# Sketched attention and a two-layer feed-forward stage: a list scheduler that counts SBUF port conflicts and shifts due times, and key features in four column tiles

## The chip, the cores and the metric

The program runs on one core of a Trainium2 chip (trn2). The metric is the device time of one execution in microseconds (us); the kernel before has a median of 130.67 us over 3 runs (130.46 to 130.88). Engines are named as the profile names them: PE is TensorE (PEld its weight loads), DVE is VectorE, ACT is ScalarE, POOL is GpSimd, SP is SyncE, which issues the DMAs.

## The reference

Attention without a softmax: queries and keys go through two 8x32 sketches S1 and S2, and the 64 features of a row are all products of the two sketched vectors. Keys and values are summed into a 64x32 matrix per head, and queries are multiplied by it and divided by the same product with the sum of the key features. The result, 4352 rows of 128, goes through a feed-forward stage of width 2048 whose activation is linear on both sides of zero.

```python
batch, n_heads, seq, head_dim = (4, 4, 1088, 32)      # r = 8
def phi(x):
    a = np.einsum('rd,bhsd->bhsr', S1, x)
    b = np.einsum('rd,bhsd->bhsr', S2, x)
    return np.einsum('bhsi,bhsj->bhsij', a, b).reshape(*x.shape[:-1], r * r)
kv  = np.einsum('bhsf,bhsd->bhfd', phi(k), v)
z   = np.sum(phi(k), axis=2)
num = np.einsum('bhsf,bhfd->bhsd', phi(q), kv)
den = np.einsum('bhsf,bhf->bhs', phi(q), z)[..., None] + 1e-06
x   = (num / den).transpose(0, 2, 1, 3).reshape(4352, 128)
h   = x @ w_in                                        # 128 x 2048
out = (np.maximum(h, 0) + alpha * np.minimum(h, 0)) @ w_out
```

The kernel rewrites the last line: with w_b = alpha * w_out and w_a = w_out - w_b, the output is relu(h) @ w_a + x @ W, where W = w_in @ w_b.

## The kernel before, in words

The kernel doesn't issue its work in program order. It first collects some hundreds of operations (`Op`, L35: a candidate engine or several, a planned duration in ns, operations it depends on, buffers it holds, a due time), then `plan` (L54) orders them, and the loop at L766 emits them in the planned order. Each engine runs its own list strictly in that order; semaphores between engines are put in where data or buffers need them, and nowhere else.

`plan` works backwards once: an operation's due time is at most that of each user, less 1.6 times its duration and latency (L62 to L64). Then it goes forwards: among the operations whose inputs are placed and whose buffers can be had, it takes on each engine the one with the earliest due time that can start within a few hundred ns (`AHEAD`) of the earliest start, and of these the one that starts first. Two engines never hinder each other in this plan, except by data and buffers.

Stages, by the names and lines that matter here:

- **Dummies.** Five matmuls on zeros (`warm`, L343) start the PE. Until the first matmul of the feed-forward stage is due, the emitting loop also fills planned gaps on the PE with such dummies, one for each 216 ns of gap less 150 ns (L769).
- **Keys** (`keys`, L485, and `kfeat`, L442), four batches, each in two halves of two heads. A half's keys are transposed (batch 0 on PE, L451; the others on DVE, L493), the features a and b come from four matmuls with the transposed keys as 128x128 weights and the block-diagonal sketches as 64 moving columns (`fe`, L460, operation "ab"), they are copied from PSUM to SBUF ("abc", L221 on ACT or L223 on DVE), and their products ("kp", L473) are formed on POOL, or on DVE for the first half of batch 0 and for the two sets of the last 64 rows (`k_rest`, L478). Then `kv` (L506: 32 matmuls with 32-column weights, L513, and small ones, L521) and `kvr` (L524) sum keys times values, and `zm`, `fin`, `zz` (L538 to L562) make kvW and zc.
- **Queries** (`queries`, L566), four batches and the last rows ("qr"): a DVE transpose (L570), two rounds of 16 matmuls (L584), copies by ACT (aq), products on DVE (L597), then denominators and numerators (L611), a transpose (L620), eps and reciprocal (`rc`, L626 and L627), a transpose (L629) and the product that gives xT (L634). Batch 0 does this in two parts, so that the feed-forward stage can start on the first.
- **Weights** (L387 to L434): w_in is cast to bf16 in four pieces; for each of four pieces of w_out, w_b is made on ACT (L404) or POOL (L395), w_a on POOL (L395), a bf16 copy of w_b ("w_hi", L223) and its remainder ("w_lo", L395) on DVE; winT (L420) and 32 matmuls (`Wmm`, L431) give W.
- **Feed-forward** (`mlp`, L685), eight groups of 512 rows and a last one of 256 (the last rows of all batches): for each of 16 chunks a matmul h (L694), a relu from PSUM to bf16 on ACT (L700) or DVE (L702), and a matmul o (L712) that accumulates in PSUM bank 7; at the end W (L708) into the same bank, an output transpose (L718, for the last group L730) and stores by SP. h takes at most four PSUM banks, the relu outputs eight buffers. Group g is due at 17 us + g * 10.2 us, chunk c of it 0.64 us later each.

DMA loads are issued by SP in one fixed order (L296 to L314): k0, q0, v0, the last rows of k and v of batches 0 and 1, k1, w_in, w_out, and then the other batches.

Of the kernel before, what the change touches and what calls it, by code (L numbers as in the profile page):

```python
# [25 lines left out]
class Buf:  # L26
# [3 lines left out]
    def __init__(self, cls, n=1, stream=None, most=99, prefer=None):  # L30
        self.cls, self.n, self.stream, self.most, self.prefer = cls, n, stream or cls, most, prefer
        self.slot, self.users, self.last = None, 0, 0.0


class Op:  # L35
    def __init__(self, eng, dur, emit, deps=(), bufs=(), lat=0, due=1e9, name=""):
        self.eng = (eng,) if isinstance(eng, str) else tuple(eng)
        self.dur = dur if isinstance(dur, dict) else {e: dur for e in self.eng}
        self.emit, self.bufs, self.lat, self.due, self.name = emit, list(bufs), lat, due, name
        self.deps = [d for d in deps if d is not None]  # L40
        self.start = self.end = self.on = None
        self.arrive = 0.0
        for b in self.bufs:
            b.users += 1
# [6 lines left out]
AHEAD = {"pe": 120, "act": 150, "dve": 250, "pool": 300, "sp": 0}  # L51


def plan(ops, classes):  # L54

    free_at = {e: 0.0 for o in ops for e in o.eng}
    freed = {c: [0.0] * n for c, n in classes.items()}
    held = {c: [False] * n for c, n in classes.items()}  # L60
    holds = {b.stream: 0 for o in ops for b in o.bufs}
    for o in reversed(ops):  # L62
        for d in o.deps:
            d.due = min(d.due, o.due - STRETCH * (min(d.dur.values()) + (0 if d.eng == o.eng == ("pe",) else d.lat + SEM)))  # L64
    waiting = sorted(ops, key=lambda o: o.due)
    order = []

    def place(o, ready):
# [24 lines left out]

    while waiting:
        shut, can = set(), []
        for o in waiting:
            new = {b.stream for b in o.bufs if b.slot is None}
            no = new & shut or any(d.end is None for d in o.deps)
            shut |= new
            if no:  # L100
                continue
            at, picks = place(o, min(max([free_at[e]] + [d.end for d in o.deps]) for e in o.eng))
            if picks is None:
                continue
            fits = []
            for e in o.eng:
                t = max([at, free_at[e]] + [d.end + SEM if d.on != e else d.free if e == "pe" else d.end + OWN for d in o.deps])
                fits.append((t + o.dur[e] * BIAS.get(e, 1), t, e))
            _, t, e = min(fits)
            end = t + o.dur[e]  # L110
            can.append((t, e, o, end, picks))
        assert can
        first, best = {}, {}
        for c in can:
            first[c[1]] = min(first.get(c[1], 1e18), c[0])
        for c in can:
            if c[0] <= first[c[1]] + AHEAD[c[1]]:
                best.setdefault(c[1], c)
        t, e, o, end, picks = min(best.values(), key=lambda c: c[0])
        for b, i in picks:  # L120
            b.slot = i
            holds[b.stream] += b.n
            for j in range(i, i + b.n):
                held[b.cls][j] = True
        o.free = end
        o.start, o.end, o.on = t, max(end + o.lat, o.arrive), e
        free_at[e] = end
        for b in o.bufs:
            b.users -= 1
            b.last = max(b.last, o.end)  # L130
            if not b.users:
                holds[b.stream] -= b.n
                for j in range(b.slot, b.slot + b.n):
                    held[b.cls][j] = False
                    freed[b.cls][j] = b.last + SEM
        waiting.remove(o)
        order.append(o)
    return sorted(order, key=lambda o: o.start)
# [3 lines left out]
def kernel(  # L142
# [52 lines left out]
    def ps(b):  # L195
        return PS[:, b.slot] if b.n == 1 else PS[:, b.slot:b.slot + b.n]
# [8 lines left out]
    def op(*a, **kw):  # L205
        o = Op(*a, **kw)
        ops.append(o)
        return o
# [107 lines left out]
    def got(name):  # L316
        return loads[name]
# [69 lines left out]
    for i in range(NP):  # L387
        s = slice(CP * i, CP * i + CP)

        def wc(e, s=s):  # L390
            copy(e, w_in_bf[:, s.start * 128:s.stop * 128], w_in_f[:, s.start * 128:s.stop * 128])
        c_win.append(op(("act", "dve"), {"act": 615, "dve": 350}, wc, got("w_in"), name="w_in_bf"))

    def tt(out, a, b, what):
        return lambda e: (nc.vector if e == "dve" else nc.gpsimd).tensor_tensor(out=out, in0=a, in1=b, op=what)  # L395
# [1 line left out]
    for i in range(NP):  # L397
        s = slice(CP * i, CP * i + CP)
        al = bview(alphaT[:, s], [[1, CP], [0, DM]])

        def wbe(e, s=s, al=al):
            if e == "act":
                for c in range(s.start, s.stop):
                    nc.scalar.activation(w_b_f[:, c], w_out_f[:, c], ACTF.Copy, scale=alphaT[:, c:c + 1])  # L404
            else:
                tt(w_b_f[:, s], w_out_f[:, s], al, ALU.mult)(e)
        wb = op(("act", "pool"), {"act": 1560, **big}, wbe, [c_S] + got("w_out"), name="w_b")
        c_wa.append(op("pool", big, tt(w_a_bf[:, s], w_out_f[:, s], w_b_f[:, s], ALU.subtract), [wb], name="w_a"))
        hi = op(("act", "dve"), {"act": 615, "dve": 350}, lambda e, s=s: copy(e, w_hl[:, 0, s], w_b_f[:, s]), [wb], name="w_hi")
        c_lo.append(op(("dve", "pool"), big, tt(w_hl[:, 1, s], w_b_f[:, s], w_hl[:, 0, s], ALU.subtract), [hi], name="w_lo"))  # L410
    for i in range(2):
        b = ph()
        s = slice(8 * i, 8 * i + 8)
# [28 lines left out]
    def kfeat(srcs, needs, due, ab_t, kp_t, bab, bkp, kp_eng, tag, turn=None):  # L442
# [14 lines left out]

        def fe(e):
            for j in range(n):
                nc.tensor.matmul(ps(bf)[:, j * 64:(j + 1) * 64], sb(bT)[:, j * 128:(j + 1) * 128],  # L460
                                 S12blk.rearrange("p h c -> p (h c)"), start=True, stop=True)
        o = op("pe", 225 * n, fe, [o, c_S], [bT, bf], 200, due + 2, tag + "ab")
        o = op(("act", "dve"), ad(64 * n),
               lambda e: copy(e, bview(ab_t(), [[r, n * H], [r * n * H, 2], [1, r]]),
                              bview(ps(bf), [[2 * r, n * H], [r, 2], [1, r]])), [o], [bf] + bab, LA, due + 3, tag + "abc")
# [1 line left out]
        def pr(e):  # L467
            a = ab_t()
            m = n * H
            dst = bview(kp_t(), [[R, m], [r, r], [1, r]])  # L470
            i0 = bview(a, [[r, m], [1, r], [0, r]])
            i1 = bass.AP(tensor=a.tensor, offset=a.offset + r * m, ap=[list(a.ap[0]), [r, m], [0, r], [1, r]])
            (nc.vector if e == "dve" else nc.gpsimd).tensor_tensor(out=dst, in0=i0, in1=i1, op=ALU.mult)  # L473
        return op(kp_eng, {"dve": dv(256 * n), "pool": 110 + 256 * n * 1.8}, pr, [o], bab + bkp, 80, due + 4, tag + "kp")

    rest_k = [None, None]

# [7 lines left out]
    def keys(b, due, kp_eng):  # L485
# [52 lines left out]
        def zm(e):  # L538
# [3 lines left out]
                                 bview(H4, [[1, 4], [0, r]]))  # L542
            nc.vector.tensor_reduce(out=u, in_=bview(t, [[1, r], [r, 4]]), axis=AX.X, op=ALU.add)
            nc.vector.tensor_mul(bview(w, [[r, H], [1, r]]), bview(u, [[0, H], [1, r]]), bview(mask4, [[1, H], [0, r]]))
        o1 = op("dve", 300, zm, [o, c_mask2], [bk, bz], 80, due + 31, f"zm{b}")
        o2 = op(("act", "dve"), ad(128), lambda e: copy(e, sb(bs), bview(ps(bk), [[0, 2], [1, R]])), [o1], [bk, bs], LA,
                due + 32, f"kvc{b}")

# [17 lines left out]
    def queries(tag, needs, due, qsrc, nf, moving, bs, nums, ncol, xmul, bx, parts=1):  # L566
# [34 lines left out]
        for part in range(parts):  # L601
# [21 lines left out]
            def rc(e, dt=dt, nb=nb):  # L623
# [1 line left out]
                u = sb(dt)[:, :nb, 1]  # L625
                nc.vector.tensor_scalar_add(t, t, EPS)  # L626
                nc.vector.reciprocal(u, t)  # L627
            o = op("dve", 250 + 8 * nb / 0.96, rc, [o], [dt], 80, name=tag + "rc")
            o = op("dve", dv(nn), lambda e, dt=dt, rr=rr, nn=nn, nb=nb: nc.vector.transpose(  # L629
                sb(rr)[:, :nn], bview(sb(dt)[:, :, 1], [[32, nb], [0, 32]])), [o], [dt, rr], 80, name=tag + "rr")  # L630
            for g in range(2) if parts == 1 else [part]:
# [134 lines left out]
    for o in done:  # L766
        if o.on == "pe":
            if o.start < first:
                dummy(max(0, int((o.start - t - 150) / 216)))  # L769
            t = o.start + o.dur["pe"]  # L770
        o.emit(o.on)

# [29 lines left out]
```

## Time and profile before

| | us |
|---|---|
| median of 3 runs | 130.67 (130.46 to 130.88) |
| the profiled execution, its own time | 131.18 |
| span in its profile | 129.4 |
| PE busy | 112.9 (87%) |
| PEld busy | 54.3 (42%) |
| DVE busy | 83.6 (65%) |
| ACT busy | 79.4 (61%) |
| POOL busy | 22.7 (18%) |

The profiled execution takes 1.78 us more than its span, and 0.51 us more than the median. Busy times are sums over instructions; a matmul counts as busy from its start to its modelled end, so matmuls that follow each other closely overlap in them. In the chain that ended last, PE has 69% of the span and DVE 17%. The time runs in three parts: the head, in which loads, features and the first queries are worked through until the first h matmul at 22.65 us; the feed-forward stage, with the keys and queries of later batches in between, until 122 us; and the last output and its store, until 129.4 us.

### The profile page before, as it was taken

The page shows a single profiled execution, that of the slowest core. Times are in us where ns is not written, and L with a number is a line of the kernel's source. Part 1 is how long each engine was busy: PE and PEld are TensorE (multiplying, and loading weights), DVE is VectorE, ACT ScalarE, POOL GpSimd, SP SyncE. Part 2 cuts the span into 40 slices and gives each one's busy share as a digit, 9 for nine tenths or more (in the row PEclk, how much of TensorE's full clock was granted, in tenths as well). Part 3 has the DMA queues.
Part 4 walks back from the last instruction along what each step waited for, and adds up shares of the span by engine and source line. Part 5 has one row for each costly group of instructions (what it writes and reads, how often), then busy time and mean ns, then how long its engine had stood idle before and what let it go on. Part 6 is the DMA issues. An engine that isn't in the chain of part 4 may idle for free.

```text
span 129.4 us, 3045 instructions
## 1 busy us (share of the span) xinstructions
PE 112.9 (87%) x1212; PEld 54.3 (42%) x1228; DVE 83.6 (65%) x148; ACT 79.4 (61%) x157; POOL 22.7 (18%) x20
## 2 busy tenths in 40 slices
PE   6997993980999999999999999999999999998800
PEld 2565371350763543355353253643233433445500
DVE  3174799999984789785665884265987535566300
ACT  3335274593078459568887568884766888765610
POOL 3025029992000083000006006000000000000000
PEclk9999998599599999999999999999999999999975
DMA  3999995699900022022004001300040310401300
GB/s 117 258 308 359 298 273 101 211 283 326 189 12 3 5 49 35 0 45 42 0 4 82 1 0 29 57 0 0 11 75 0 60 23 0 84 3 25 61 14 26
DMA packets 32322, 11.22 MB, mean 87 GB/s; under 512 B 26788, under 2 KB 31668, under 8 KB 32180
## 3 DMA queue, kind: packets, MB, share of 16 engines
q1 hardware_dynamic: 32196, 11.01, 35.1%
q8 instruction: 9, 0.15, 0.5%
q14 instruction: 5, 0.04, 0.1%
q10 hardware_dynamic: 112, 0.02, 0.1%
HBM read 8.80 MB, written 2.23 MB: 85 GB/s over the span
## 4 chain that ended last, share of the span: by engine, by line
PE 69%; DVE 17%; ACT 5%; issue 2%; POOL 2%; DVEq 0%; ACTq 0%
PE ps L712 20%; PE ps L694 20%; PE ps L584 6%; PE ps L611 6%; PE ps L460 5%; PE ps L513 4%; DVE aq__76 L597 4%; DVE w_hl L223 3%; PE ps L342 3%; POOL kp__71 L473 2%; DVE w_hl L395 2%; ACT rh__83 L700 2%; PE ps L431 1%; ACT rh__82 L700 1%; PE ps L708 1%
## 5 line engine op out<-in xcount | busy, mean ns | idle before, releaser
L694 PE MATMUL ps<-xT__94,w_in_bf 128*128 128x512 bf16 (+1 forms) x78 | 27.4, 376 | 3.1 <-DVE xT__94 L634 2.3
L700 ACT ACTIVATE rh__82<-ps 128x512 bf16<-128x512 f32 (+1 forms) x37 | 21.3, 575 | 13.2 <-PE ps L694 12.7
L694 PEld LDWEIGHTS <-w_in_bf 128*128 128x128 bf16 x144 | 14.2, 100 | 22.8 <-issue 11.1
L694 PE MATMUL ps<-xT__95,w_in_bf 128*128 128x512 bf16 x62 | 23.2, 379 | 0.1
L700 ACT ACTIVATE rh__84<-ps 128x512 bf16<-128x512 f32 (+1 forms) x29 | 16.5, 570 | 8.1 <-PE ps L694 8.0
L712 PEld LDWEIGHTS <-w_a_bf 128*128 128x128 bf16 x144 | 14.3, 101 | 16.8 <-issue 4.5
L700 ACT ACTIVATE rh__83<-ps 128x512 bf16<-128x512 f32 (+1 forms) x32 | 18.2, 569 | 3.5 <-PE ps L694 1.9
L712 PE MATMUL ps<-rh__84,w_a_bf 128*128 128x512 bf16 (+1 forms) x37 | 13.8, 372 | 3.6 <-DVE rh__84 L702 3.5
L712 PE MATMUL ps<-rh__82,w_a_bf 128*128 128x512 bf16 (+1 forms) x38 | 14.2, 374 | 0.1
L712 PE MATMUL ps<-rh__83,w_a_bf 128*128 128x512 bf16 (+1 forms) x38 | 14.1, 370 | 0.1
L473 POOL TENSOR_TENSOR kp__70<-ab__67 128x1024 f32<-128x1024 f32 x3 | 5.9, 1955 | 41.3 <-DVE ab__67 L223 18.2
L702 DVE TENSOR_SCALAR rh__84<-ps 128x512 bf16<-128x512 f32 x10 | 6.9, 690 | 6.9 <-PE ps L694 6.8
L473 POOL TENSOR_TENSOR kp__71<-ab__68 128x1024 f32<-128x1024 f32 x4 | 8.5, 2130 | 15.5 <-ACT ab__68 L221 15.5
L597 DVE TENSOR_TENSOR aq__76<-ps,aq__76 128x1024 f32<-128x1024 f32 (+1 forms) x8 | 8.0, 1018 | 3.0 <-PE ps L584 3.0
L718 DVE STREAM_TRANSPOSE oT__91<-ps 128x512 f32<-128x512 f32 x8 | 5.7, 716 | 3.8 <-PE ps L708 3.6
L342 PE MATMUL ps<-zero 128*128 128x512 bf16 x19 | 6.8, 494 | 1.4 <-DVE tab L334 1.2
L221 ACT COPY aq__76<-ps 128x1024 f32<-128x1024 f32 (+1 forms) x8 | 6.6, 853 | 2.2 <-PE ps L584 2.2
L700 ACT ACTIVATE rh__85<-ps 128x512 bf16<-128x512 f32 x10 | 6.0, 598 | 3.2 <-PE ps L694 3.1
L702 DVE TENSOR_SCALAR rh__83<-ps 128x512 bf16<-128x512 f32 x9 | 6.1, 681 | 2.3 <-PE ps L694 2.2
L584 PE MATMUL ps<-qT__74,Sab 32*64 32x512 f32 x96 | 6.8, 624 | 0.0
L513 PEld LDWEIGHTS ps<-kp__70,v 128*32 128x32 f32 x128 | 4.5, 124 | 5.4 <-issue 5.0
L620 DVE STREAM_TRANSPOSE dt__78<-ps 128x1024 f32<-128x1024 f32 (+2 forms) x6 | 5.6, 933 | 0.9 <-PE ps L611 0.9
(119 smaller groups left out, 171.1 us busy)
## 6 DMA issues: line engine op xcount, KB each, us to landing
out_dram<-oT__91 SPq DMA_DIRECT2D x34, 64.0 KB, 1.9
q<-in_q_dram SPq DMA_DIRECT2D x4, 512.0 KB, 5.6
k<-in_k_dram SPq DMA_DIRECT2D x3, 512.0 KB, 5.2
v<-in_v_dram SPq DMA_DIRECT2D x12, 128.0 KB, 5.2
w_in_f<-in_moe_w_in_dram SPq DMA_DIRECT2D x1, 1024.0 KB, 8.9
k<-in_k_dram SPq DMA_DIRECT2D x2, 256.0 KB, 2.8
v<-in_v_dram SPq DMA_DIRECT2D x1, 512.0 KB, 6.7
kr<-in_k_dram SPq DMA_DIRECT2D x4, 32.0 KB, 4.2
```

What stands on the lines that cost most here:

```text
L221: nc.scalar.copy(dst, src)
L342: nc.tensor.matmul(PS[:, 7], zero[:, :128], zero, start=True, stop=True, skip_group_check=True)
L460: nc.tensor.matmul(ps(bf)[:, j * 64:(j + 1) * 64], sb(bT)[:, j * 128:(j + 1) * 128], S12blk.rearrange("p h c -> p (h c)"), start=True, sto ...
L473: (nc.vector if e == "dve" else nc.gpsimd).tensor_tensor(out=dst, in0=i0, in1=i1, op=ALU.mult)
L513: nc.tensor.matmul(ps(bk)[32 * h:32 * h + 32, :R], v_sb[b][:, h, 4 * x + t if pe else 2 * t + x], bview(kp[h // 2], [[1, 1024]])[:, ((2 * ...
L584: nc.tensor.matmul(dst, bview(Sab[32 * t:32 * t + 32, i], [[1, R]]), moving(sb(bq), t, c), start=True, stop=True)
L597: nc.vector.tensor_mul(a, told(ps(b2[x])[:, :, :nf]), a)
L611: nc.tensor.matmul(dst, w, mv, start=True, stop=True, skip_group_check=True)
L694: nc.tensor.matmul(ps(b)[:, :n], w_in_bf[:, c * 128:(c + 1) * 128], xs(), start=True, stop=True)
L700: nc.scalar.activation(sb(br)[:, :n], ps(b)[:, :n], ACTF.Relu)
L702: nc.vector.tensor_scalar_max(sb(br)[:, :n], ps(b)[:, :n], 0.0)
L712: nc.tensor.matmul(ps(bo)[:, :n], w_a_bf[:, c], sb(hs[c][1])[:, :n], start=c == 0, stop=False)
```

## The change

Four things change in one step.

1. `Op` gets a flag `port`. It is set on DVE's casts of w_in and w_b, on w_lo, on `zm` and on `rc`. In `plan`, an operation placed on POOL may not start before the end of the last flagged operation on DVE, and a flagged operation on DVE not before the end of the last operation on POOL. Nothing in the emitted program enforces this: it changes the order only.
2. After the backward pass, a table `SHIFT` of 116 names adds a fixed number of ns to due times: -235 for most h matmuls in the middle of the groups, -5,700 to -11,200 for the query operations of batch 3 and of the last rows, -2,000 to -3,600 for those of the keys of batch 2, -1,355 for w_b, -3,584 for w_hi, +2,650 for Wmm, and others.
3. `fe` splits each feature matmul into four with 32-column weights, one for each group of 32 output partitions, and its planned time falls from 225n to 175n + 30 ns.
4. Where the key products run on DVE, their first factor is read from the feature bank in PSUM and no longer from its copy in SBUF; that bank is then held until the products are done.

The emitting loop now counts one dummy for each 430 ns of gap, and no longer for each 216 ns, where the following operation is planned before 9 us.

```diff
+SHIFT = {
+    "W2": 1677, "W3": -1622, "W4": 6669, "W6": -6660, "W7": 3243, "Wmm": 2650, "h0.10": -235, "h0.6": -235,
...
+    "h8.7": -235, "h8.8": -235, "h8.9": -235, "k0.0Tc": -1099, "k0.1abc": -774, "k1.1abc": 1627,
+    "k1.1kp": 932, "k2.0T": -2020, "k2.0ab": -3558, "k2.0abc": -3377, "k2.0kp": -2903, "k2.1T": -3578,
...
+    "q0b": 538, "q1x": -327, "q3T": -11216, "q3a": -6003, "q3ac": -7606, "q3b": -6929, "q3dT": -8045,
+    "q3den": -9018, "q3num": -7121, "q3rr": -7727, "qrT": -6857, "qra": -6091, "qrac": -6079, "qrb": -5966,
+    "qrdT": -6858, "qrden": -6121, "qrnum": -5687, "qrrr": -7529, "r7.5": -80, "w_b": -1355, "w_hi": -3584,
+    "winT": -1925,
+}
...
     free_at = {e: 0.0 for o in ops for e in o.eng}
+    free_at["port"] = 0.0
...
+    for o in ops:
+        o.due += SHIFT.get(o.name, 0)
     waiting = sorted(ops, key=lambda o: o.due)
...
+                if e == "pool":
+                    t = max(t, free_at["port"])
+                elif e == "dve" and o.port:
+                    t = max(t, free_at["pool"])
...
+        if e == "dve" and o.port:
+            free_at["port"] = end
...
         def fe(e):
             for j in range(n):
-                nc.tensor.matmul(ps(bf)[:, j * 64:(j + 1) * 64], sb(bT)[:, j * 128:(j + 1) * 128],
-                                 S12blk.rearrange("p h c -> p (h c)"), start=True, stop=True)
-        o = op("pe", 225 * n, fe, [o, c_S], [bT, bf], 200, due + 2, tag + "ab")
+                for i in range(4):
+                    nc.tensor.matmul(ps(bf)[32 * i:32 * i + 32, j * 64:(j + 1) * 64],
+                                     sb(bT)[:, j * 128 + 32 * i:j * 128 + 32 * i + 32],
+                                     S12blk.rearrange("p h c -> p (h c)"), start=True, stop=True)
+        o = op("pe", 175 * n + 30, fe, [o, c_S], [bT, bf], 200, due + 2, tag + "ab")
...
-            i0 = bview(a, [[r, m], [1, r], [0, r]])
+            i0 = bview(a, [[r, m], [1, r], [0, r]]) if e == "pool" else bview(ps(bf), [[2 * r, m], [1, r], [0, r]])
...
-                dummy(max(0, int((o.start - t - 150) / 216)))
+                dummy(max(0, int((o.start - t - 150) / (430 if o.start < 9000 else 216))))
```

## Rows read from the trace of the kernel before

**Rows 1.** The page's second part: busy share and PE clock, 40 slices

```profile
PE   6997993980999999999999999999999999998800
PEclk9999998599599999999999999999999999999975
```

**Rows 2.** Stretches: us; busy of PE, PEld, DVE, ACT, POOL; PEclk, DMA share, GB/s

```profile
5.00:20.50 15.50, 14.24 (x234) 9.01 (x235) 10.97 (x22) 8.27 (x20) 4.43 (x2) 1.00 1.00 302
...
20.48:22.65 2.17, 0.00 (x1) 0.01 (x1) 1.96 (x5) 0.51 (x2) 2.17 (x3) 0.84 0.42 69
22.65:25.50 2.85, 2.85 (x7) 1.04 (x8) 2.85 (x5) 1.70 (x3) 2.85 (x4) 0.52 0.59 192
28.70:32.20 3.50, 0.04 (x2) 0.00 (x0) 3.50 (x6) 1.39 (x3) 1.33 (x1) 1.00 1.13 316
32.20:35.50 3.30, 3.30 (x90) 2.32 (x97) 3.20 (x7) 0.09 (x1) 0.00 (x0) 0.50 1.14 198
36.00:80.00 44.00, 43.54 (x456) 20.20 (x447) 31.15 (x54) 30.86 (x60) 7.63 (x4) 1.00 0.11 19
```

**Rows 3.** DVE in order of time, 19 to 34 us: start, duration, what

```profile
19.39 1.34 DVE L626 TENSOR_SCALAR dt__78<-dt__78 128x16 f32<-128x16 f32 x1
...
25.54 3.38 DVE L223 CAST w_hl<-w_b_f 128x512 bf16<-128x512 f32 x2
28.84 1.75 DVE L395 TENSOR_TENSOR w_hl<-w_b_f,w_hl 128x512 bf16<-128x512 f32 x1
30.51 0.41 DVE L223 CAST w_hl<-w_b_f 128x512 bf16<-128x512 f32 x1
30.84 0.68 DVE L395 TENSOR_TENSOR w_hl<-w_b_f,w_hl 128x512 bf16<-128x512 f32 x1
31.44 0.68 DVE L702 TENSOR_SCALAR rh__84<-ps 128x512 bf16<-128x512 f32 x1
...
33.98 0.18 DVE L626 TENSOR_SCALAR dt__78<-dt__78 128x16 f32<-128x16 f32 x1
```

**Rows 4.** POOL in order of time, 8 to 32 us

```profile
8.83 2.66 POOL L473 TENSOR_TENSOR kp__71<-ab__68 128x1024 f32<-128x1024 f32 x1 [7.17 <-ACT ab__68 L221]
18.73 1.95 POOL L473 TENSOR_TENSOR kp__70<-ab__67 128x1024 f32<-128x1024 f32 x1 [7.24 <-DVE aq__76 L597]
...
24.09 1.22 POOL L395 TENSOR_TENSOR w_b_f<-w_out_f,S12T 128x512 f32<-128x512 f32 x1
25.28 1.95 POOL L473 TENSOR_TENSOR kp__71<-ab__68 128x1024 f32<-128x1024 f32 x1
27.18 2.85 POOL L395 TENSOR_TENSOR w_a_bf<-w_out_f,w_b_f 128x512 bf16<-128x512 f32 x2
```

**Rows 5.** PE in order of time: the stall's end, the first dummies, the first o

```profile
1.19 3.93 PE L342 MATMUL ps<-zero 128*128 128x512 bf16 x9 [1.19 <-DVE tab L334]
...
24.75 0.63 PE L712 MATMUL ps<-rh__82,w_a_bf 128*128 128x512 bf16 x1
...
32.17 0.58 PE L712 MATMUL ps<-rh__84,w_a_bf 128*128 128x512 bf16 x1 [3.46 <-DVE rh__84 L702]
```

**Rows 6.** ACT, the first reader of w_out

```profile
18.54 0.70 ACT L404 ACTIVATE w_b_f<-w_out_f,S12T 128x128 f32<-128x128 f32 x2
```

**Rows 7.** The chain of waits, 45 to 57 us: a feature product, and L513

```profile
45.53 0.84 PE ps L460 x8
...
55.84 0.21 PE ps L694
56.05 1.03 PE ps L513 x64
```

**Rows 8.** PE in order of time, the change from wide to 32-column weights

```profile
55.67 0.38 PE L694 MATMUL ps<-xT__95,w_in_bf 128*128 128x512 bf16 x1
55.98 0.25 PE L513 MATMUL ps<-kp__70,v 128*32 128x64 f32 x2
```

**Rows 9.** PE in order of time, around the queries of batch 3 and the last rows

```profile
89.95 1.93 PE L694 MATMUL ps<-xT__94,w_in_bf 128*128 128x512 bf16 x6
92.11 1.09 PE L611 MATMUL ps<-aq__76,zc 64*32 64x512 f32 x16 [0.24 <-DVE zc L561]
```

More of the change, by code (lines that the diff above doesn't have):

```diff
@@ L35, with __init__ @@
 class Op:
-    def __init__(self, eng, dur, emit, deps=(), bufs=(), lat=0, due=1e9, name=""):
+    def __init__(self, eng, dur, emit, deps=(), bufs=(), lat=0, due=1e9, name="", port=False):
         self.eng = (eng,) if isinstance(eng, str) else tuple(eng)
@@ L39, in __init__ @@
         self.emit, self.bufs, self.lat, self.due, self.name = emit, list(bufs), lat, due, name
+        self.port = port
         self.deps = [d for d in deps if d is not None]
@@ L391, in wc @@
             copy(e, w_in_bf[:, s.start * 128:s.stop * 128], w_in_f[:, s.start * 128:s.stop * 128])
-        c_win.append(op(("act", "dve"), {"act": 615, "dve": 350}, wc, got("w_in"), name="w_in_bf"))
+        c_win.append(op(("act", "dve"), {"act": 615, "dve": 350}, wc, got("w_in"), name="w_in_bf", port=True))
     def tt(out, a, b, what):
@@ L408 @@
         c_wa.append(op("pool", big, tt(w_a_bf[:, s], w_out_f[:, s], w_b_f[:, s], ALU.subtract), [wb], name="w_a"))
-        hi = op(("act", "dve"), {"act": 615, "dve": 350}, lambda e, s=s: copy(e, w_hl[:, 0, s], w_b_f[:, s]), [wb], name="w_hi")
-        c_lo.append(op(("dve", "pool"), big, tt(w_hl[:, 1, s], w_b_f[:, s], w_hl[:, 0, s], ALU.subtract), [hi], name="w_lo"))
+        hi = op(("act", "dve"), {"act": 615, "dve": 350}, lambda e, s=s: copy(e, w_hl[:, 0, s], w_b_f[:, s]), [wb], name="w_hi", port=True)
+        c_lo.append(op(("dve", "pool"), big, tt(w_hl[:, 1, s], w_b_f[:, s], w_hl[:, 0, s], ALU.subtract), [hi], name="w_lo", port=True))
     for i in range(2):
@@ L470, in pr @@
             dst = bview(kp_t(), [[R, m], [r, r], [1, r]])
-            i0 = bview(a, [[r, m], [1, r], [0, r]])
+            i0 = bview(a, [[r, m], [1, r], [0, r]]) if e == "pool" else bview(ps(bf), [[2 * r, m], [1, r], [0, r]])
             i1 = bass.AP(tensor=a.tensor, offset=a.offset + r * m, ap=[list(a.ap[0]), [r, m], [0, r], [1, r]])
             (nc.vector if e == "dve" else nc.gpsimd).tensor_tensor(out=dst, in0=i0, in1=i1, op=ALU.mult)
-        return op(kp_eng, {"dve": dv(256 * n), "pool": 110 + 256 * n * 1.8}, pr, [o], bab + bkp, 80, due + 4, tag + "kp")
+        return op(kp_eng, {"dve": dv(256 * n), "pool": 110 + 256 * n * 1.8}, pr, [o],
+                  bab + bkp + ([bf] if kp_eng == "dve" else []), 80, due + 4, tag + "kp")
     rest_k = [None, None]
@@ L544, in zm @@
             nc.vector.tensor_mul(bview(w, [[r, H], [1, r]]), bview(u, [[0, H], [1, r]]), bview(mask4, [[1, H], [0, r]]))
-        o1 = op("dve", 300, zm, [o, c_mask2], [bk, bz], 80, due + 31, f"zm{b}")
+        o1 = op("dve", 300, zm, [o, c_mask2], [bk, bz], 80, due + 31, f"zm{b}", True)
         o2 = op(("act", "dve"), ad(128), lambda e: copy(e, sb(bs), bview(ps(bk), [[0, 2], [1, R]])), [o1], [bk, bs], LA,
@@ L627, in rc @@
                 nc.vector.reciprocal(u, t)
-            o = op("dve", 250 + 8 * nb / 0.96, rc, [o], [dt], 80, name=tag + "rc")
+            o = op("dve", 250 + 8 * nb / 0.96, rc, [o], [dt], 80, name=tag + "rc", port=True)
             o = op("dve", dv(nn), lambda e, dt=dt, rr=rr, nn=nn, nb=nb: nc.vector.transpose(
```

9 rows, old and new, of the table SHIFT are left out of this document.

## The prediction

> **What bounds the kernel now.** I read the page's slices first. PE is at nine tenths in nearly all of them; the slices that fall short lie before slice 11 (about 35 us), and so do two dips of the clock to 0.5 [rows 1]. So I read the stretches next. From 36 to 80 us PE is busy 43.54 of 44.00 us at a granted clock of 1.00, with DVE and ACT at about 31 us each [rows 2]: there only less PE work helps. What can be won lies mostly in the head and in its two pauses: 20.48 to 22.65 us, where PE does nothing and then runs 2.85 us at 0.52, and 28.70 to 32.20 us, where PE is busy 0.04 of 3.50 us and then runs 3.30 us at 0.50 [rows 2]. A clock of 0.5 is the 1.2 GHz level, 1.00 the 2.4 GHz one, and both falls come right behind a pause of the engine.
>
> Both pauses end with DVE, so I read DVE and POOL beside each other. The eps addition of `rc` takes 1.34 us at 19.39 and 0.18 us at 33.98 for the same shape [rows 3]; the first ends at 20.73, where POOL's product that began at 18.73 has just ended (20.68) [rows 4]. Two casts take 3.38 us where one later takes 0.41, and a w_lo takes 1.75 us where the next takes 0.68 [rows 3]; in that time POOL is never idle [rows 4]. So these DVE instructions stand still until a POOL instruction lets go. Behind them on DVE's list stands the relu of rh at 31.44 [rows 3], and the o matmul that needs it resumes PE after 3.46 us [rows 5]. The plan gave the casts 350 ns and knew of none of this.
>
> **The change, part by part,** as gains against the profiled 131.18 us (span 129.4, 1.78 around it).
>
> *The port flag, relu stall.* From 25.54 to 31.44 DVE spends 5.90 us on three casts and two w_lo [rows 3]; at their unhindered 0.41 and 0.68 us they would take 2.6, so 3.3 us are blocking. With the flag they are planned after POOL, and a relu can go ahead. Ends 0 and 3.46 (the whole idle [rows 5]); I take 3.0, nearest to the blocking. *The clock behind it:* 3.30 us at 0.50 [rows 2] cost 1.65; without the pause, 1.6 (ends 0 and 1.65).
>
> *The port flag, `rc`.* 1.34 less 0.18 is 1.16 us on the path to xT and the first h: 1.15 (ends 0 and 1.16). *The clock after it:* 2.85 us at 0.52 cost 1.4 [rows 2]; about 1 us of pause stays, though where the plan sees a gap it fills it with dummies. No row shows a pause of that length by itself, so I take the middle: 0.7 (ends 0 and 1.4).
>
> *The start.* Nine dummies take 3.93 us, 0.44 each [rows 5], and the key transposes stand behind them. Five are fixed; of the other four, a divisor of 430 in place of 216 drops two: 0.87. The products of batch 0: POOL's takes 2.66 us instead of 1.95 [rows 4], because DVE's own, with both inputs in SBUF, runs beside it; with one factor in PSUM it should not hold POOL: 0.7 on the way to kv0. That the feature bank is held longer on three products costs nothing: in those 1.2 us only the first query round (four banks) and kv0 (one) want others of the eight. The features of batch 0 add 0.4 (below). Together 2.0. But o cannot start before w_a, nor w_a before w_out, first read at 18.54 [rows 6]; with a w_b of 1.22 and a w_a of 1.4 [rows 4] that is 21.2, against 24.75 now [rows 5], and `rc` and the clock already use half of those 3.6 us. I take 1.0 (ends 0 and 2.0).
>
> *Four column tiles.* A feature product of eight PE instructions takes 0.84 us; kv, with 64 instructions of the new shape (32-column weights, 64 moving columns, fp32), takes 1.03 us [rows 7]. The new product has 32, so 0.52: a gain of 0.32. Going over from wide weights costs something: L513 starts 0.31 us after the h before it [rows 8] where h and o follow each other at 0.21 [rows 7], so 0.1. That leaves 0.22 for each of the four large products of batches 2 and 3, which lie in the PE-bound stage, and a little for the second set of last rows: 0.9. The upper end is 1.3, without the 0.1. The lower: if these small loads fail to run beside each other as well as kv's, which change head at each step, a product takes as long as now plus 0.1, a loss of 0.5. The Trainium skill, TensorEngine Tiling (Array Packing), Key Properties, speaks against this part: a change of tiling mode drains the engine. The trace agrees with a pause at entry [rows 8]; by that rule a second pause at the exit would bring the term from 0.9 to 0.5, and no row here shows one.
>
> *Due-time shifts.* The queries of batch 3 and of the last rows come forward by 6 to 11 us. Now, six h in a row wait for DVE and take 2.16 us [rows 9] instead of 6 x 0.216 = 1.3, since DVE works at that query's products: 0.86 lost, of which I take 0.5 (ends 0 and 0.86). In the last group I take 0.4, half of the same 0.86 as the nearest row (ends 0 and 0.9): xT of the last rows is then ready early. The -235 ns on h move each h before the o of three chunks back; PE runs the same matmuls, and 43.54 of 44.00 us leave nothing to gain [rows 2]: nothing. No DMA is added or moved, so SP's queue stays as it is.
>
> Sum: 3.0 + 1.6 + 1.15 + 0.7 + 1.0 + 0.9 + 0.5 + 0.4 = 9.25 us.
>
> *What is given back.* POOL works from 18.73 to 30.03 without a break [rows 4]: 11.3 us. DVE's flagged work there (four casts, four w_lo, `rc`, at unhindered durations) is 4 x 0.41 + 4 x 0.68 + 0.2 = 4.6 us. If it must stand between POOL's operations, the last w_a, for which the o of group 0's last chunks wait, can come up to 4.6 us later, while the o that need it come 2 to 3 us earlier. w_hi is drawn forward, so some of it will: 1.5 us, a third (ends 0 and 4.6). A new order also has its own small jams; the one row of such a thing is the 0.86 above, and I take one and a half of them, 1.25 (ends 0 and 2.6). Net 9.25 - 2.75 = 6.5 us.
>
> 131.18 - 6.5 = 124.7 for a profiled execution; the median stood 0.51 below it, so **124.2 us**.
>
> **The rivals.** (1) *The lock moves instead of going.* The planned order holds only if POOL and DVE start when the plan says; no semaphore stands between them. If POOL begins a product just ahead of a flagged DVE instruction, that one blocks again, with relus behind it, or POOL's w_a comes late and o waits. Then the 3.0 and the 1.6 are lost and half of the `rc` terms (0.9): 9.25 - 5.5 - 1.25 = 2.5, so 128.2 us. For it: by today's plan DVE ran into POOL four times in 12 us (`rc`, two casts, a w_lo [rows 3, 4]). Against: w_hi and w_lo are due late and the plan lets other work go first. The Trainium skill, SBUF — State Buffer, Who interferes with whom, says issue order decides who is blocked, for the whole instruction; the trace agrees, with `rc` ending 0.05 us after POOL's product. Chance 0.19.
>
> (2) *Slower: the clock falls in the head.* Fewer dummies leave PE with pauses before 9 us. Now the stretch from 5 to 20.5 us runs at 1.00 with PE busy 14.24 us [rows 2]. If it fell to 0.5 there, PE's work would double; some 3.5 us of it are dummies, of the other 10.7 I take two thirds as lying on the way to xT, the rest beside loads and DVE work: 7 us later. The terms of the start and of `rc` are lost too: 9.25 - 2.85 - 2.75 = 3.65 gained, 7 lost: 134.0 us. It decides the sign once more than half of that stretch runs at the lower level. Against: only two or so of the dummies go. Chance 0.06.
>
> (3) *More is won.* The given-back terms vanish and the start gains in full: 131.18 - 0.51 - 10.25 = 120.4 us. For it: the plan now knows the blocking, and the stage from 36 us is dense already. Chance 0.17.
>
> (4) *Nothing comes of it.* The order of the stall hardly changes, since deps and buffers set it: the features, the last queries and half the start give 2.3, the jams and a later w_a take it: 130.7. Chance 0.04.
>
> **How the numbers follow.** Forecast 0.54, rivals 0.19, 0.06, 0.17, 0.04. The range takes in rivals 1 and nearly all of 3 and leaves out 2 and 4 and the far corners of the bounds: 120.0 to 129.0 us. About 0.3% of 130.67, 0.4 us, is what a measurement can tell from no change. Rival 1 stays faster in most of its bounds, 4 is the same for the most part. Faster 0.88, same 0.04, slower 0.08.
>
> **What would show it.** Right: `rc`, the casts and w_lo near 0.2, 0.4 and 0.7 us, no PE pause over 1 us between the first h and 36 us, a clock of 1.00 in 28 to 36 us, the POOL product of batch 0 at 1.95 us, feature products near 0.5 us, no run of six h near the queries of batch 3. Wrong: a cast or w_lo still over 1 us with a relu behind it, o waiting for w_a from POOL, a clock near 0.5 before 20 us, feature products at 0.8 us or more.

## The result and the profile after

The kernel after takes 124.48 us (median of 4 runs, 123.16 to 125.16), the one before 130.77 (130.46 to 131.11): the ratio is 0.9485, 95% interval 0.9399 to 0.9571. The forecast was 124.2 us. Executions more than 1.5% longer than a kernel's fastest are left out of every ratio and of the differences in us below; where the median without them differs, it stands in parentheses behind the median, for the kernel after 124.48 us (124.12). The profiled execution of the kernel after is the fastest of its four, 123.16 us, with a span of 121.4, 8.0 less than that of before. That total hides two errors that cancel, so the stages come first.

The page's second part of the kernel after, busy share of PE and PE clock in 40 slices of 3.04 us:

```profile
PE   6969289599999999999999999999999999999700
PEclk9999968999999999999999999999999999999995
```

Stretches of the kernel after, with the columns of [rows 2]:

```profile
12.85:15.57 2.72, 0.00 (x1) 0.12 (x3) 1.22 (x1) 0.00 (x0) 0.00 (x0) 1.00 1.05 296
15.57:20.70 5.13, 4.97 (x103) 3.05 (x103) 3.09 (x6) 2.97 (x8) 1.95 (x1) 0.67 0.94 205
...
22.90:28.00 5.10, 4.91 (x105) 2.98 (x108) 5.10 (x8) 4.26 (x10) 5.10 (x5) 1.00 1.17 309
28.00:36.00 8.00, 7.57 (x111) 4.04 (x108) 7.86 (x16) 5.70 (x13) 3.30 (x3) 1.00 0.85 205
```

Against [rows 1, 2], the pause at 28.70 us is gone, and so are both stretches at 0.5: behind the first h the granted clock is 1.00, the 2.4 GHz level. In their place stands a pause that before did not have, 12.85 to 15.57 us, with a clock of 0.67 on average behind it. The first h therefore starts at 22.90 us and not earlier than before (22.65); the last wide matmuls are over, and ACT takes the last output, at 114.28 us and not 122.26. All of the gain lies between those two (122.26 - 22.65 = 99.61 us before, 114.28 - 22.90 = 91.38 after, 8.2 less); the head won nothing.

The chain that ended last, kernel after (start, us, what), first the new pause, then w_lo on DVE, then a feature product between two h of the feed-forward stage:

```profile
11.81 1.04 PE ps L618 x16
12.85 2.72 issue
15.57 0.81 PE ps L373 x2
...
28.72 3.73 DVE w_hl L426 x3
32.45 1.01 DVE kT__64 L527 x2
...
39.60 0.22 PE ps L728
39.82 0.58 PE ps L492 x32
40.40 0.32 PE ps L728
```

"issue" says that PE waited for nothing that the profile shows: the next instruction is a dummy on zeros. The product takes 0.58 us where it took 0.84 [rows 7], and the h behind it 0.32 in place of 0.22. The same chain in the kernel before has the h behind the whole product, and the o behind kv, whose weights have 32 columns:

```profile
46.37 0.22 PE ps L694
...
57.21 0.32 PE ps L712
```

DVE, POOL and ACT in order of time, kernel after, answering to [rows 3, 4]:

```profile
20.76 0.16 DVE L660 TENSOR_SCALAR dt__78<-dt__78 128x16 f32<-128x16 f32 x1
...
28.05 0.67 DVE L736 TENSOR_SCALAR rh__83<-ps 128x512 bf16<-128x512 f32 x1
28.65 3.80 DVE L426 TENSOR_TENSOR w_hl<-w_b_f,w_hl 128x512 bf16<-128x512 f32 x3
```
```profile
7.96 1.95 POOL L506 TENSOR_TENSOR kp__71<-ab__67 128x1024 f32<-128x1024 f32 x1 [6.30 <-ACT ab__67 L252]
...
28.35 2.95 POOL L426 TENSOR_TENSOR w_a_bf<-w_out_f,w_b_f 128x512 bf16<-128x512 f32 x2
```
```profile
24.02 1.13 ACT L252 CAST w_hl<-w_b_f 128x512 bf16<-128x512 f32 x2
...
27.03 1.13 ACT L252 CAST w_hl<-w_b_f 128x512 bf16<-128x512 f32 x2
...
28.96 0.60 ACT L734 ACTIVATE rh__84<-ps 128x512 bf16<-128x512 f32 x1
...
32.32 0.65 ACT L734 ACTIVATE rh__89<-ps 128x512 bf16<-128x512 f32 x1
```

`rc` is free (0.16 us), POOL's product of batch 0 takes 1.95 us, and the w_hi casts have left DVE for ACT. But three w_lo still take 3.80 us beside POOL's w_a, almost twice the 0.68 each of [rows 3]. The blocking is still there; what changed is that no relu is lost behind it, since ACT evicts eight of them from 28.96 us on. It even lies in the chain that ended last, from 28.72 us on, with key transposes behind it, but PE is busy 7.57 of the 8.00 us from 28 to 36 us.

So three questions stood open: which part removed the stall, what the new pause is, and what the splits and the start are worth.

### The profile page after: what moved, and what is told of

Read it like the earlier page. It is cut to its first block, busy times and chain, and to the rows that moved or that the text cites. A ratio compares the mean times of both kernels' runs of the same rounds, so it can differ in the third digit from the quotient of the medians.

```text
span 121.4 us, 3418 instructions
## 1 busy us (share of the span) xinstructions
PE 106.3 (88%) x1409; PEld 50.7 (42%) x1426; DVE 81.6 (67%) x147; ACT 79.6 (66%) x157; POOL 23.1 (19%) x21
## 4 chain that ended last, share of the span: by engine, by line
PE 70%; DVE 13%; DMA 4%; issue 4%; ACT 2%; SPq 1%; DVEq 0%
PE ps L728 23%; PE ps L746 22%; PE ps L645 7%; PE ps L618 7%; DMA q<-in_q_dram 4%; DVE w_hl L426 3%; PE ps L492 3%; PE ps L547 2%; PE ps L742 2%; DVE rr__80 L663 1%; DVE dt__78 L654 1%; DVE rh__83 L736 1%; DVE qT__74 L604 1%; PE ps L373 1%; DVE aq__76 L631 1%
## 5 line engine op out<-in xcount | busy, mean ns | idle before, releaser
L728 PE MATMUL ps<-xT__94,w_in_bf 128*128 128x512 bf16 (+1 forms) x78 | 26.4, 357 | 1.8 <-DVE xT__94 L668 1.3
L728 PE MATMUL ps<-xT__95,w_in_bf 128*128 128x512 bf16 x63 | 23.7, 380 | 0.2
L746 PEld LDWEIGHTS <-w_a_bf 128*128 128x128 bf16 x144 | 13.7, 97 | 16.4 <-issue 3.5
L734 ACT ACTIVATE rh__82<-ps 128x512 bf16<-128x512 f32 (+1 forms) x28 | 16.1, 575 | 6.0 <-PE ps L728 5.7
L734 ACT ACTIVATE rh__83<-ps 128x512 bf16<-128x512 f32 (+1 forms) x28 | 16.3, 581 | 4.9 <-PE ps L728 4.6
L734 ACT ACTIVATE rh__84<-ps 128x512 bf16<-128x512 f32 (+1 forms) x26 | 14.9, 572 | 2.2 <-PE ps L728 1.8
L734 ACT ACTIVATE rh__85<-ps 128x512 bf16<-128x512 f32 (+1 forms) x19 | 11.1, 586 | 4.4 <-PE ps L728 2.9
L746 PE MATMUL ps<-rh__82,w_a_bf 128*128 128x512 bf16 (+1 forms) x35 | 13.0, 371 | 0.2 <-DVE rh__83 L736 0.2
L746 PE MATMUL ps<-rh__83,w_a_bf 128*128 128x512 bf16 (+1 forms) x33 | 12.2, 370 | 0.3 <-issue 0.3
L746 PE MATMUL ps<-rh__84,w_a_bf 128*128 128x512 bf16 (+1 forms) x31 | 11.4, 368 | 0.0
L506 POOL TENSOR_TENSOR kp__70<-ab__67 128x1024 f32<-128x1024 f32 x2 | 3.9, 1951 | 34.7 <-ACT ab__67 L252 34.7
L746 PE MATMUL ps<-rh__85,w_a_bf 128*128 128x512 bf16 (+1 forms) x25 | 9.3, 371 | 0.0
L373 PE MATMUL ps<-zero 128*128 128x512 bf16 x13 | 5.2, 531 | 4.1 <-issue 2.9
L736 DVE TENSOR_SCALAR rh__82<-ps 128x512 bf16<-128x512 f32 x9 | 6.2, 689 | 3.6 <-PE ps L728 3.6
L736 DVE TENSOR_SCALAR rh__85<-ps 128x512 bf16<-128x512 f32 (+1 forms) x8 | 5.2, 656 | 2.9 <-PE ps L728 2.9
L736 DVE TENSOR_SCALAR rh__84<-ps 128x512 bf16<-128x512 f32 x7 | 4.8, 690 | 2.7 <-PE ps L728 2.7
L736 DVE TENSOR_SCALAR rh__83<-ps 128x512 bf16<-128x512 f32 (+1 forms) x8 | 5.2, 654 | 1.9 <-PE ps L728 1.7
```

What stands on the lines that cost most here:

```text
L373: nc.tensor.matmul(PS[:, 7], zero[:, :128], zero, start=True, stop=True, skip_group_check=True)
L728: nc.tensor.matmul(ps(b)[:, :n], w_in_bf[:, c * 128:(c + 1) * 128], xs(), start=True, stop=True)
L734: nc.scalar.activation(sb(br)[:, :n], ps(b)[:, :n], ACTF.Relu)
L736: nc.vector.tensor_scalar_max(sb(br)[:, :n], ps(b)[:, :n], 0.0)
L746: nc.tensor.matmul(ps(bo)[:, :n], w_a_bf[:, c], sb(hs[c][1])[:, :n], start=c == 0, stop=False)
```

## The experiments

Four kernels take one part alone or leave one part out.

**The port flag alone** (`port` and its rule in `plan`, on the kernel before):

```diff
...
+                if e == "pool":
+                    t = max(t, free_at["port"])
+                elif e == "dve" and o.port:
+                    t = max(t, free_at["pool"])
...
```

> The kernel before with the port flag and its two rules in the plan, nothing else. Theory (the gain is mostly blocked DVE work that the plan now steps around): the stall of 3.46 us before the o at 32.17 and the 1.34 us eps addition go, with a third given back, so about 126.5 us (125.5 to 128). Rival (the flag alone only moves the blocking; the shifts carry the gain): 129.5 to 131.5, with casts or w_lo over 1 us and a relu behind them.

Measured: 130.99 us, ratio 0.9982 (0.9945 to 1.0018), no change. My theory, that the flag carries the gain, missed. DVE of this kernel in order of time, and PE at its first h and at its longest wait behind it:

```profile
24.90 1.63 DVE L231 CAST w_hl<-w_b_f 128x512 bf16<-128x512 f32 x1
26.45 4.65 DVE L403 TENSOR_TENSOR w_hl<-w_b_f,w_hl 128x512 bf16<-128x512 f32 x4
```
```profile
25.04 0.39 PE L702 MATMUL ps<-xT__94,w_in_bf 128*128 128x512 bf16 x1 [0.20 <-DVE xT__94 L642]
...
34.01 0.38 PE L702 MATMUL ps<-xT__94,w_in_bf 128*128 128x512 bf16 x1 [1.62 <-DVE xT__94 L642]
```

The time hides two shifts. The stall of 3.46 us is gone, the longest wait behind the first h is 1.62 us, and the stretch from the first h until ACT takes the last output is 2.9 us shorter (96.75 us, 99.61 before). But the first h comes 2.4 us later (25.04 us): the eps addition, whose input is there at 19.55 us, starts at 22.76 (before at 19.39 [rows 3]), as the rule holds it behind POOL's work in the plan. And four w_lo still meet POOL's w_a: a planned order without a semaphore does not keep two engines apart.

**The due-time shifts alone** (the table, on the kernel before):

```diff
...
+    for o in ops:
+        o.due += SHIFT.get(o.name, 0)
```

> The kernel before with the table of due-time shifts alone. Theory: the plan still doesn't know of the blocking, so casts and w_lo still take over 1 us somewhere; the last queries come earlier for 0.9 us at most: 129 to 131. Rival (the shifts carry the gain): 125 to 127.5.

Measured: 128.16 us (127.06), ratio 0.9684 (0.9571 to 0.9796), better than theory, short of the rival. In its profiled execution, one of 128.38 us, PE still waits for a relu that stands behind blocked casts on DVE:

```profile
31.51 0.38 PE L734 MATMUL ps<-rh__82,w_a_bf 128*128 128x512 bf16 x1 [2.03 <-DVE rh__82 L724]
```
```profile
28.28 2.58 DVE L245 CAST w_hl<-w_b_f 128x512 bf16<-128x512 f32 x2
30.78 0.68 DVE L724 TENSOR_SCALAR rh__82<-ps 128x512 bf16<-128x512 f32 x1
```

**All features whole** (the kernel after, in its order, each feature product as before):

```diff
-                for i in range(4):
-                    nc.tensor.matmul(ps(bf)[32 * i:32 * i + 32, j * 64:(j + 1) * 64],
...
+                nc.tensor.matmul(ps(bf)[:, j * 64:(j + 1) * 64], sb(bT)[:, j * 128:(j + 1) * 128],
...
```

> The kernel after in its own order, with every feature matmul whole again (128-column weights). Two theories on the PE pause of 2.72 us at 12.85 us, in which it waits for nothing that the profile shows. Instructions: the split adds 272 matmuls and loads to PE's list, 108 of them before the pause, and PE runs out of fetched instructions; whole, the pause goes and the first h comes up to 2 us earlier, against 0.3 us for each of ten products: 123.5 to 124.5, no pause over 0.5 us near 13 us. Rival (the pause belongs to the order, for example to the dummies there): the pause of 2 to 3 us stays, and 1 to 2 us are lost on the products: 125.5 to 126.5.

Measured: 121.01 us, ratio 0.9229 (0.9164 to 0.9293): taking the part out makes the kernel faster, by 3.1 us and by more than I expected. The pause at 13 us is gone and the first h starts at 19.86 us.

**Only the late features split** (the kernel after; batches 0 and 1 and the first last rows whole):

```diff
+                if tag[:2] in ("k0", "k1") or tag == "kr0":
+                    nc.tensor.matmul(ps(bf)[:, j * 64:(j + 1) * 64], sb(bT)[:, j * 128:(j + 1) * 128],
+                                     S12blk.rearrange("p h c -> p (h c)"), start=True, stop=True)
+                    continue
```

> The kernel after in its own order, features of batches 0 and 1 whole, those of batches 2 and 3 and of their last rows in four tiles. Instructions: the pause at 12.85 us goes while the gain of 0.22 us for each late product stays: 122 to 123.5. Rival (the pause belongs to the order): 124.5 to 125.5 with a pause of 2 to 3 us.

Measured: 120.40 us, ratio 0.9181 (0.9128 to 0.9234): the best version here, below the range that I expected and 3.7 us under the kernel after, whose interval it does not touch. Against the version with all features whole it is 0.6 us better, but those intervals overlap, so this 0.6 is not shown by the times. Its PE in order of time:

```profile
12.34 1.11 PE L622 MATMUL ps<-qT__74,Sab 32*64 32x512 f32 x16
13.61 0.59 PE L373 MATMUL ps<-zero 128*128 128x512 bf16 x2 [0.16 <-issue]
...
18.29 0.59 PE L373 MATMUL ps<-zero 128*128 128x512 bf16 x2 [0.85 <-issue]
18.81 0.66 PE L649 MATMUL ps<-aq__76,zc 64*32 64x256 f32 x16
19.97 0.38 PE L732 MATMUL ps<-xT__94,w_in_bf 128*128 128x512 bf16 x1 [0.49 <-DVE xT__94 L672]
```

The place of the pause (behind the second query round) now passes at 13.61 us, and the first h comes 2.9 us earlier than in the kernel after. This version is the base of the next runs, called the base (in the expectations e4_split_late_only).

**The base without the shifts** (`SHIFT` not applied):

```diff
-        o.due += SHIFT.get(o.name, 0)
+        pass
```

> e4_split_late_only with the shifts left out of the plan (port flag, products from PSUM, late features in four tiles, one dummy for 430 ns kept). After the first job the flag alone gave nothing and the shifts alone 3.2%. Theory now (the two only work together: the flag makes the plan see the blocking, the shifts decide what gives way): 126 to 130 us, with the casts or w_lo on DVE in front of relus in 25 to 35 us. Rival (the shifts only trim the end): 121.5 to 124.

Measured: 128.13 us, ratio 0.9816 (0.9743 to 0.9889). **The base without the port rule** (both branches in `plan` left out):

```diff
-                    t = max(t, free_at["port"])
-                elif e == "dve" and o.port:
-                    t = max(t, free_at["pool"])
+                    pass
```

> e4_split_late_only without the two port rules in the plan, shifts kept. Theory (both needed): 124 to 128 us, a cast or the eps addition over 1 us on the way to the first h, and a PE pause over 1 us before 36 us. Rival (the shifts alone order the work well, the flag adds nothing): 120 to 121.5.

Measured: 126.33 us (125.39), ratio 0.9589 (0.9501 to 0.9676). Both times came as expected. One sign did not: without the shifts no relu stands behind the casts and w_lo on DVE. The first h of each, PE in order of time, without the shifts and then without the port rule:

```profile
23.21 1.23 PE L732 MATMUL ps<-xT__94,w_in_bf 128*128 128x512 bf16 x3 [3.50 <-DVE xT__94 L672]
```
```profile
19.57 1.44 PE L730 MATMUL ps<-xT__94,w_in_bf 128*128 128x512 bf16 x3 [2.46 <-DVE xT__94 L670]
```

The second starts as early as the base but after 2.46 us without work, and PE then runs at the lower level; that kernel's stretch from 20 to 25 us, and a cast that blocks again:

```profile
20.00:25.00 5.00, 5.00 (x39) 2.56 (x38) 5.00 (x7) 2.84 (x7) 5.00 (x5) 0.50 0.55 141
```
```profile
23.55 2.74 DVE L252 CAST w_hl<-w_b_f 128x512 bf16<-128x512 f32 x2
```

So the two parts need each other: on the kernel before the flag gives nothing and the table 4.1 us (131.17 for the kernel before in the same runs, less 127.06), while on the base losing the table costs 7.7 us and losing the flag 5.0. They do not add up. The traces tell where:

| | first h, us | from there until ACT takes the last output, us |
|---|---|---|
| before | 22.65 | 99.61 |
| flag alone | 25.04 | 96.75 |
| table alone | 23.72 | 95.82 |
| base | 19.97 | 91.64 |
| base without the table | 23.21 | 95.83 |
| base without the flag | 19.57 | 96.73 |

Either part alone shortens the feed-forward stage, and makes the first h later. Taken from the base, the table costs 3.2 us ahead of the first h and 4.2 behind it; the flag costs 5.1 us, all of it behind.

Two kernels move the split to find what the pause at 12.85 us hangs on. **Only batch 0 split early** and **only batch 1 and the first last rows split early** (besides the late ones):

```diff
-                if tag[:2] in ("k0", "k1") or tag == "kr0":
+                if tag[:2] == "k1" or tag == "kr0":
```
```diff
-                if tag[:2] in ("k0", "k1") or tag == "kr0":
+                if tag[:2] == "k0":
```

> e4_split_late_only with the two products of batch 0 in four tiles as well, so that PE's list has 96 more instructions ahead of the place of the pause (429 in place of 333; the kernel after had 440). Instructions: a PE pause of 1.5 to 2.7 us behind the second query round, before 16 us, and 122.5 to 124.5 us. Rival (the four tiles themselves, or their place in batch 1, made the pause): no such pause, 119.5 to 120.5.

> e4_split_late_only with the products of batch 1 and of the first last rows in four tiles as well, batch 0 whole: 108 more PE instructions than in e4_split_late_only, but 96 of them behind the place of the pause. Instructions: no pause over 0.5 us behind the second query round; one may come later, 120 to 121.5 us. Rival (it is the number of split products before the first h that counts, wherever they stand): 122.5 to 124.5 with a pause of 1.5 to 2.7 us.

Measured: 122.19 us (121.21), ratio 0.9269 (0.9179 to 0.9359), and 124.49 us (124.05), ratio 0.9488 (0.9397 to 0.9579). The first has the pause, but its time is a little below my range; its trace is of an execution of 122.81 us. The second missed what I expected: a pause came there too, at another place, in the middle of a run of equal matmuls that wait for no data. PE in order of time, first and second kernel:

```profile
16.74 0.44 PE L492 MATMUL ps<-S12blk,kT__64 128*128 128x64 f32 x3 [2.11 <-issue]
```
```profile
17.75 0.46 PE L649 MATMUL ps<-aq__76,zc 64*32 64x256 f32 x3 [2.08 <-issue]
```

What is equal is the count. Stretches from 0 to just ahead of the resumption; the numbers behind x are instructions of PE and PEld: the kernel after, then these two:

```profile
0.00:15.50 15.50, 10.68 (x219) 5.97 (x222) 7.78 (x21) 5.50 (x9) 2.94 (x8) 1.00 0.88 285
```
```profile
0.00:16.70 16.70, 12.46 (x220) 6.89 (x221) 9.13 (x25) 5.76 (x10) 2.95 (x8) 1.00 0.89 272
```
```profile
0.00:17.70 17.70, 13.31 (x220) 7.54 (x221) 9.16 (x25) 8.21 (x15) 4.90 (x9) 1.00 0.88 279
```

In the latter two PE stops after 441 of its instructions. In the kernel after it is 440: the 441st counted is the weight load at 15.35 us that ends the pause, and its trace lacks some matmuls (1409 against 1426 weight loads). So I put instructions there without splitting anything. **Small dummies**: the base, with the two dummies ahead of `fin0` replaced by 56 small matmuls on zeros:

```diff
+                if o.name == "fin0":
+                    for _ in range(56):
+                        nc.tensor.matmul(PS[:32, 7, :32], zero[:32, :32], zero[:32, :32], start=True, stop=True,
+                                         skip_group_check=True)
...
```

> The version with whole early features (120.40 us, first h at 19.97), with its two dummies at 13.61 us replaced by 56 matmuls of 32x32 weights and 32 columns on zeros: no feature is split that was not split before, and no data wait is added; only about 108 instructions of PE and PEld more stand between 12.3 and 15 us. Theory (PE runs out of instructions after its 441st, and gets the next ones about 7 us after it has passed its 180th, here at 11.39): a pause at the small ones' end or at the matmuls just behind them, over 2 us, ending between 18.0 and 19.2; first h at 22.2 to 23.5; 122.7 to 124.3 us. Rival (the pause comes of the split features themselves, their narrow weights or the changes of tile shape): only the small matmuls' own time, under 1.5 us; first h at 20 to 21.3; 120.4 to 121.6 us.

Measured: 127.59 us, ratio 0.9723 (0.9637 to 0.9808). PE in order of time, and the count:

```profile
12.72 1.51 PE L809 MATMUL ps<-zero 32*32 32x32 bf16 x54
17.34 0.20 PE L809 MATMUL ps<-zero 32*32 32x32 bf16 x2 [3.10 <-issue]
```
```profile
0.00:17.20 17.20, 12.54 (x220) 7.69 (x221) 7.89 (x21) 5.50 (x9) 2.94 (x8) 1.00 0.93 287
```

PE stops between two equal small matmuls, once more after 220 + 221 = 441 instructions. No feature is split here that the base has whole, so the rival's split features fall. These small matmuls have narrow weights too; what speaks against narrow weights and tile shapes is that the stop comes in the middle of a run of equal ones, and that in the two kernels above it comes at the same count ahead of a whole feature and among the denominators. The pause began and ended earlier than I wrote (the small ones started at 12.72, not 13.61 us), and the time is 3.3 us above my range: behind the pause PE ran from 20 to 25 us at a clock of 0.50, and the first h came at 25.99 us.

Two kernels undo a part of the start, on the base. **Products from SBUF** (the bank still held, the order kept):

```diff
-            i0 = bview(a, [[r, m], [1, r], [0, r]]) if e == "pool" else bview(ps(bf), [[2 * r, m], [1, r], [0, r]])
+            i0 = bview(a, [[r, m], [1, r], [0, r]])
```

> The version with whole early features (120.40 us), with the key products on DVE read from SBUF again; the feature bank is held as before, so the order of all instructions stays. My step: POOL's product of batch 0 goes back from 1.95 to about 2.66 us, and kv0, first h and the end move by 0.5 to 0.9 us: 120.9 to 121.3 us. Rival: POOL's product is slower, but kv0 waits for the last rows' product or the transposes at that time, so nothing is lost: 120.2 to 120.6 us.

Measured: 121.71 us (121.66), ratio 0.9292 (0.9200 to 0.9384), 1.3 us over the base and a little above my range. DVE and POOL in order of time:

```profile
8.59 2.81 DVE L510 TENSOR_TENSOR kp__70<-ab__68 128x1024 f32<-128x1024 f32 x1 [0.37 <-ACT ab__68 L252]
11.32 0.28 DVE L254 COPY kT__64<-ps 128x128 f32<-128x128 f32 x1
```
```profile
8.36 1.95 POOL L510 TENSOR_TENSOR kp__71<-ab__67 128x1024 f32<-128x1024 f32 x1 [6.70 <-ACT ab__67 L252]
```

POOL started first this time and keeps its 1.95 us; DVE, 0.23 us later, stands until POOL is done and takes 2.81 us, and the copy that PE needs next slips behind it. The first h comes at 21.15 us, 1.18 us later than in the base. My step had the cost on POOL; it falls on whoever starts second.

**More dummies** (216 ns for each, before 9 us too):

```diff
-                dummy(max(0, int((o.start - t - 150) / (430 if o.start < 9000 else 216))))
+                dummy(max(0, int((o.start - t - 150) / 216)))
```

> The version with whole early features (120.40 us), with the dummies before 9 us counted by 216 ns again: nine at the start in place of seven. My step: the key transposes begin about 0.87 us later and all behind them moves by 0.4 to 0.9 us: 120.8 to 121.3 us. Rival: the first queries' DVE transpose waits for its load until about 7.0 us anyway, so the later key transposes are hidden: 120.2 to 120.6 us.

Measured: 121.45 us, ratio 0.9276 (0.9217 to 0.9335), 1.05 us over the base, and also just above my range. PE in order of time:

```profile
1.19 4.02 PE L373 MATMUL ps<-zero 128*128 128x512 bf16 x9 [1.19 <-DVE tab L365]
...
20.61 1.02 PE L732 MATMUL ps<-xT__94,w_in_bf 128*128 128x512 bf16 x4 [0.57 <-DVE xT__94 L672]
```

The first h is 0.64 us later than the base's 19.97, the first o 1.07 (23.65 against 22.58); the query load hides only part of the two dummies. For both of these the intervals overlap the base's (0.9128 to 0.9234); the traces carry the sizes.

## Why the prediction was right in its number

The number held (124.48 against 124.2), the sign too. That it fits so closely is luck. The prediction had 2.15 us won ahead of the first h (`rc` and the start) and 4.35 behind it (7.1 less the 2.75 given back); the traces show 0.25 us lost ahead of it and 8.2 won behind it. By its steps:

- **The relu stall (3.0) and the clock behind it (1.6): right in size, the cause only in part.** Both are gone; together they held 3.46 + 1.65 = 5.1 us [rows 5, 2]. The step said: "With the flag they are planned after POOL, and a relu can go ahead." That held in part. With the flag alone the relu stall is gone, but PE is still idle for 2.85 of the 9.00 us from 25 to 34 us, w_lo blocks as before, and the first h comes 2.4 us later, a price of the flag that the prediction put at nothing; the time stays. The runs show that the gain needs flag and table together. In the trace of the kernel after the w_hi casts are on ACT and ACT takes the relus while three w_lo take 3.80 us on DVE. That this is the way in which it works was read from the trace, not tried by itself.
- **`rc` (1.15) and the clock after it (0.7).** `rc` takes 0.16 us, and behind the first h the clock is 1.00: right where they stand. Without the flag `rc` is back at 1.09 us and the dip at 0.50 too. What `rc` won ahead of the first h went into the new pause. A lower clock in the head, the sign of rival 2, did come (0.67 behind the pause), but not from fewer dummies: the base has the same dummies and runs at 1.00 from 15 to 20 us.
- **The start (1.0): failed.** The first h came 0.25 us later. Its parts were there: in the base seven dummies for nine are worth 1.05 us, the product from PSUM 1.3, and in the base the first h is 2.7 us and the first o 2.2 us earlier (22.58 against 24.75). The step that failed is "The features of batch 0 add 0.4": split early, they bring the pause of 2.72 us. I costed the time of the added instructions, not their number.
- **Four column tiles (0.9): the product right, the sum not.** 0.58 us measured, 0.52 and 0.1 for the entry forecast. The h behind it takes 0.32 us in place of 0.22, so one product gains 0.84 + 0.22 - 0.58 - 0.32 = 0.16, four of them 0.64; from the first h on the kernel after is 0.66 us shorter than the one with all features whole (91.38 against 92.04); the times of whole and late split, 0.6 us apart, do not show it. The rule of the Trainium skill that I held against this part (TensorEngine Tiling (Array Packing), Key Properties: a change of tiling mode drains the engine) named this second pause, and the trace agrees, at 0.1 us. "No row here shows one" overlooked a row: in the trace of before the o behind kv takes 0.32 us already. The early split costs 3.7 us, so the part as made loses about 3.1.
- **Shifts (0.5 + 0.4): too small.** No run of six h stands near the queries of batch 3 any more. But the table is worth far more, in what it does with the flag: 7.7 us when it is taken from the base, 3.2 of it ahead of the first h and 4.2 behind it in the trace.
- **Given back (1.5 + 1.25).** In the kernel after o waits for w_a once, for 0.2 us. What was given back went to the pause and the lower clock behind it: 2.9 us at the first h, 3.7 us by the medians, against the base.

Without the early split the time is that of rival 3, "more is won": 120.40 against 120.4 us. That it meets the number is luck again: its `rc` and start make 3.15 us ahead of the first h, and the base's first h is 2.7 us earlier. Rival 1, the lock that moves instead of going, is what the flag alone did.

## What to carry to other kernels

Where two parts of a change order the same engines, the price of one alone says little: run each alone and each left out. When a change multiplies an engine's small instructions early in a kernel, count them as well as their time, and look for an "issue" pause that keeps its count when the program around it moves. A planner's rule without a semaphore shifts who blocks whom; put the blocked work where no one waits behind it.

## What the runs showed of the hardware

**PE can run out of instructions.** Four kernels stopped for 2.1 to 3.1 us after 440 or 441 instructions of PE and PEld in their traces, whatever came next. The queue that the page calls "q8 instruction" carries 11 packets, 0.18 MB, in the kernel after. From the traces' records, in us:

| | first packet of the queue | #442 starts | pause |
|---|---|---|---|
| before | 15.82 | 18.89 | none |
| base | 15.33 | 18.29 | 0.85 |
| after | 12.87 | 15.57 | 2.72 |
| batch 0 split early | 14.06 | 16.74 | 2.11 |
| batch 1 split early | 15.11 | 17.75 | 2.08 |
| small dummies | 14.66 | 17.34 | 3.10 |

In the four that stopped, PE's next matmul starts 2.64 to 2.70 us after the packet has started; the kernel before comes to the same place 3.07 us after it and passes. The base stands there for 0.85 us, so a part of the pause may be left in the best version; no run tells. What calls for the packet, and so how fast instructions may follow each other without a stop, these runs do not show: the 180th instruction in my expectation for the small dummies was a guess, and in all the kernels here the packet comes 2.7 to 5.1 us after it. The clock behind such a pause was 0.67 in the kernel after, 0.64 with batch 1 split early, 0.50 with the small dummies, and 1.00 with batch 0 split early.

The Trainium skill, Runtime: NRT & Kernel Launch, Instruction fetch mechanics, says that instructions come in blocks of 256 through a queue of the sequencer's own and that this is mostly hidden. The trace agrees with blocks (0.18 MB in 11 packets is 16 KB each); hidden it is not, at 2.72 us. The other queues are full at that time (a DMA share of 1.04 from 5.00 to 12.80 us in the kernel after); whether the block would come sooner with fewer loads was not tried and stays open.

**The port blocks on either side.** The same pair of products cost POOL 0.7 us before (2.66 in place of 1.95 [rows 4]), where DVE's began 0.33 us earlier, and DVE 1.6 us without the product from PSUM (2.81 in place of 1.22, as the base has it), where POOL's began 0.23 us earlier.
